# P V of a decode kernel: P standing in two column tiles, V moving, the useful quarter picked by 32-bit matmuls

## The chip, the cores and the metric

The kernel runs on one core of a Trainium2 chip. The metric is device microseconds of one execution, the median of three runs; beside it stands one execution taken with the hardware profiler, whose trace gives the durations used here. TensorE is called PE (its weight loads PEld), VectorE DVE, ScalarE ACT, GpSimd POOL; SP is the engine that issues nearly all DMAs. Times in the text are in us from the start of the profiled span, if nothing else is said.

## What is computed

One decode step of a block: attention over a window of cached keys and values, and then an MLP, each with a layer norm in front of it. Eight sequences (B = 8), one token each, D = 512; 32 query heads of 128, 8 KV heads, four query heads to each; the last W = 2048 positions of the cache.

```python
W = min(4096, max(256, Sk // 4))                      # 2048
q = (x @ wq).reshape(B, 1, 32, 128)                   # per head
k = k_cache[:, :, Sk - W:, :]; v = v_cache[:, :, Sk - W:, :]   # repeated for 4 heads each
p = softmax(q k^T * 128**-0.5)
attention = (p v) @ wo
h = x + attention(layernorm(x))
out = h + mlp(layernorm(h))     # its token shift is zero for one token, so w1 and w2 are not used;
                                # mlp(y) = y + gelu(layernorm(y) @ w3) @ w4, with F = 1792
```

K and V of the window are 67 MB of the 79.2 MB that the kernel reads.

## The kernel before, in words

**Units.** A unit n is one batch element b and one half t of its KV heads: n = 2 b + t, 16 units in all. Each has J = 4 KV heads, W = 2048 positions, and 2 MB of K and 2 MB of V. In SBUF a unit's K or V is one buffer `[128, 8192]`: partition 4 r + j holds, for KV head j, 64 positions of 128 numbers. There are four such buffers for K (`knat`) and four for V (`vnat`). "Even unit" below means t = 0 and "odd unit" t = 1.

**K.** PE turns a unit's K in four steps (`turn_K`, L296: eight 32-bit transposes each, reading two bf16 numbers as one), alternating between two PSUM buffers `kT_ps`; ACT empties the lower half of each (L283) and DVE the upper half (L284). After two such steps `pe_QK` (L311) multiplies: q standing with 32 columns, K moving with 512, in four column tiles of the array, one for each KV head. The scores of a batch element fill one PSUM bank, one row for each pair of head and position group.

**Softmax.** After the odd unit: the row maximum on DVE (`softmax_1`), matmuls that bring it together over partitions and back (`softmax_2`, L325, and `softmax_3`, L336), the exponential on ACT (L342). In the next even unit `softmax_spread` (L355, four steps on DVE) spreads P over four times its width with zeros in the other KV heads' places, `softmax_5` (L372, L375, L381) makes the reciprocal sums, and `softmax_4` (L364) turns P into `pS`, so that positions lie on partitions.

**P V.** `pe_PV(i)` is a quarter w of unit n (i = 4 n + w): 16 matmuls in which a chunk of V stands (128 x 128) and 16 columns of `pS` move, all 64 of a unit adding into `oT_ps[:, 0:16]`, so that the head dimension comes out on partitions. `scale` (L407, DVE) multiplies by the reciprocal sums and spreads the result in `oK`; `turn_o` (L417, four matmuls in column tiles; L422, a copy on DVE) rearranges it into `o2`, the moving operand of the product with wo (`pe_wo`, L458).

**Order.** Each engine gets its instructions in the order in which the program emits them, and waits on counters. One pass of the main loop handles K of unit n and P V of unit n - 3 (no P V in pass 14, unit 11 in pass 15):

```python
turn_K(i); spread(0); turn_os(pv[0] // U); turn_K(i + 1); spread(1); turn_K(i + 2); spread(2)
pe_QK(2 * n)
if t == 0 and b >= 1: softmax_5(b - 1)
turn_K(i + 3); spread(3); pvs(1)
pe_QK(2 * n + 1)
if t == 0 and b >= 1: softmax_4(b - 1)
if t == 1: softmax_1(b); pvs(2); softmax_2(b); pvs(3); softmax_3(b)
pvs(4)
```

`spread` does something in even units alone, and `pvs(k)` emits P V quarters up to the k-th of its unit. So an even unit has one quarter ahead of its second QK and three together at its end; in an odd unit the four stand apart. After the loop come the spreads of the last batch element, P V of unit 12, `softmax_5`, `softmax_4`, P V of units 13 to 15 with the first half of the product with wo among them, `turn_o` of unit 15, the second half of wo, and the MLP.

**DMA.** SP issues in program order: K of unit n waits until K of unit n - 4 has been turned, V of unit n until P V of unit n - 4 is done. V of unit 15 is issued in four pieces, behind it four pieces of wo, then w3 and w4 (these two into K's buffers). `sm` is a PSUM bank that L325, L336, L372 and `turn_o` share; a variable `sm_read` makes each of them wait for the last reader of it.

Of the kernel before, what the change touches and what calls it, by code (L numbers as in the profile page):

```python
# [6 lines left out]
dt = mybir.dt  # L7
ACT = mybir.ActivationFunctionType
ALU = mybir.AluOpType
AX = mybir.AxisListType  # L10
# [3 lines left out]
H = 32  # L14
DH = 128
G = 8
R = H // G
# [11 lines left out]
NU = 2  # L29
J = G // NU  # L30
U = 4
# [5 lines left out]
NV = 4  # L37
NKT = 4
LVD = 3
WO_AT = (5, 9)  # L40
WO_G = (0, 2)
WO_L = 4
QW = 12 + R + 28
SPR = 4


# [30 lines left out]
def bass_sequential_preLN__sliding_block_cached__mixer_s_mlp__decode_kernel(  # L77
# [19 lines left out]
    NUN = NB * NU  # L97
# [4 lines left out]
    with es:  # L102
        sb = lambda shape, dtype, name: es.enter_context(nc.sbuf_tensor(name, shape, dtype))
# [4 lines left out]
        vnat = sb([128, NV, UL], dt.bfloat16, "vnat")  # L108
# [6 lines left out]
        ident_f = sb([128, 128], dt.float32, "ident_f")  # L115
# [3 lines left out]
        sel_f = sb([128, H], dt.float32, "sel_f")  # L119
# [32 lines left out]
        mK = sb([128, R], dt.float32, "mK")  # L152
        rLk = sb([128, 2, H, R], dt.float32, "rLk")
        oK = sb([128, 2, J, R, R], dt.bfloat16, "oK")
        o2 = sb([128, G, R, B], dt.bfloat16, "o2")

        NH = KC * B
        tail = Pz[:, 0, :].bitcast(dt.float32)
        at = [0]
# [30 lines left out]
        def dma(eng, dst, src, sem, *waits):  # L190
            def f(e):
# [25 lines left out]
        e_sel = DV.op(lambda e: e.tensor_reduce(sel_f[:, :].rearrange("p (j h) -> p j h", j=J),  # L217
                                                ident_f[:, :].rearrange("p (j u h) -> p j h u", j=J, u=U),
                                                AX.X, ALU.add), e_idf)
        e_mE = DV.op(lambda e: e.tensor_reduce(mE[:, :], ident_f[:, :].rearrange("p (e k) -> p e k", k=R),  # L220
                                               AX.X, ALU.max))
        e_mK = DV.op(lambda e: e.tensor_reduce(mK[:, :], ident_f[:, :].rearrange("p (e k) -> p k e", k=R),
# [41 lines left out]

        def fill_q(b):
            for c in range(2):
                at = 12 + 16 * c
                e_qw[b] = PO.op(lambda e, c=c, at=at: e.tensor_copy(  # L268
                    qz[64 * c:64 * (c + 1), b % 2, :, :, at:at + R],
                    q_sb[64 * c:64 * (c + 1), :, :, b].rearrange("p k (g h) -> p g k h", h=R)),  # L270
                    e_qs, (PO.sem, PO.count), e_QK.get(2 * (NU * (b - 2) + 1) + 1))
# [30 lines left out]
        def pe_QK(m):  # L302
            n, v = divmod(m, 2)
            b, t = divmod(n, NU)
            lo = 12 - 8 * v - 4 * t
            kT = kT_sb[:, (2 * m) % NKT:(2 * m) % NKT + 2, :].rearrange("p u (c j r k) -> p j k (u c) r", c=8, j=J, k=2)

            def f(e):
                for k in range(2):
                    for j in range(J):  # L310
                        ins = e.matmul(S_ps[b % 2][32 * j:32 * (j + 1), :].rearrange("p (c r) -> p c r", c=16),  # L311
                                       qz[:, b % 2, J * t + j, k, lo:lo + 32], kT[:, j, k],
                                       start=(t == 0 and v == 0 and k == 0), stop=(t == NU - 1 and v == 1 and k == 1),
                                       tile_position=(0, 32 * j), skip_group_check=True)
                return ins
            e_QK[m] = PE.op(f, *e_ev[2 * m], *e_ev[2 * m + 1], e_qw[b], e_qs, e_exp.get(b - 2))
# [7 lines left out]
        def softmax_2(b):  # L324
            e_mT[b] = PE.op(lambda e: e.matmul(sm[0:1, MROW], mcol[:, :], ident_f[:, :], start=True, stop=True),  # L325
                            e_max[b], sm_read[0], e_idf)
            e = DV.op(lambda e: e.tensor_reduce(Mrow[:, :].rearrange("o (j h) -> o j h", j=J),  # L327
                                                sm[0:1, MROW].rearrange("o (j u h) -> o j h u", j=J, u=U),
                                                AX.X, ALU.max), e_mT[b])
            sm_read[0] = e  # L330
            m_bc = bass.AP(tensor=Mrow[:, :].tensor, offset=0, ap=[[H, 1], [8, J], [0, U], [1, 8]])
            e_neg[b] = DV.op(lambda e: e.tensor_scalar(negrow[:, :].rearrange("o (j u h) -> o j u h", j=J, u=U), m_bc,  # L332
                                                       -1.0, None, ALU.mult), e, e_negps.get(b - 1))

        def softmax_3(b):
# [46 lines left out]

        def V(n, w):
            if n == NUN - 1:
                return sem_vl[w], 16
            return sem_v[n % NV], 16 * (n // NV + 1)

        def pe_PV(i):
            n, w = divmod(i, U)
            b, t = divmod(n, NU)  # L390
            dst = oT_ps[:, 0:16]

            def f(e):
                for c in range(16):
                    o = (8 * (w % 2) + c // 2) * 128 + 16 * (2 * (2 * (c % 2) + w // 2) + t)
                    mvg = pS[:, b % 2, o:o + 16]
                    ins = e.matmul(dst, vnat[:, n % NV, (16 * w + c) * DH:(16 * w + c + 1) * DH], mvg,  # L397
                                   start=(w == 0 and c == 0), stop=(w == U - 1 and c == 15),
                                   skip_group_check=True)
                return ins  # L400
            e_PV[i] = PE.op(f, V(n, w), *e_pS[b], e_sc.get(n - 1))

        def scale(n):
            b, t = divmod(n, NU)
            src = oT_ps[:, 0:16]
            s_bc = bass.AP(tensor=src.tensor, offset=src.offset, ap=[src.ap[0], [1, 16], [0, R]])
            e_sc[n] = DV.op(lambda e: e.tensor_tensor(oK[:, n % 2].rearrange("p g r k -> p (g r) k"), s_bc,  # L407
                                                      rLk[:, b % 2, 16 * t:16 * t + 16, :], ALU.mult),
                            e_rL[b], e_PV[U * n + U - 1], e_scale.get(n - 2))

        def turn_o(n):
            b, t = divmod(n, NU)
# [19 lines left out]
        def load_v(n):  # L432
            b, t = divmod(n, NU)
            src = A_v_cache[b, J * t:J * (t + 1), W0:SK, :].rearrange("j (r c) d -> r j (c d)", r=RR)
            if n < NUN - 1:
                dma(SP, vnat[:, n % NV, :], src, sem_v[n % NV], e_PV.get(U * (n - NV + 1) - 1))
                return
            for w in range(U):
                cs = slice(w * UL // U, (w + 1) * UL // U)
                dma(SP, vnat[:, n % NV, cs], src[:, :, cs], sem_vl[w], e_PV.get(U * (n - NV + 1) - 1))  # L440

# [32 lines left out]
        turned = [0]  # L474

        def turn_os(to):
            while turned[0] < to:
                turn_o(turned[0])
                turned[0] += 1
# [6 lines left out]
        for n in range(NUN):  # L486
            if n < NUN - 1:
                load_k(n)
            if n == NUN - 2:
                load_k(n + 1)  # L490
            if n >= LVD:
                load_v(n - LVD)
            if n in WO_AT:
                load_wo(WO_G[WO_AT.index(n)], sem_wo)
            i = U * n
            b, t = divmod(n, NU)
            lag = LVD + (n >= NUN - 2)
# [85 lines left out]
        e = PE.op(lambda e: e.matmul(st2, ones_v[:, :], vsum[:, :], start=True, stop=True), e_vs, e_sc[NUN - 1])  # L583
# [72 lines left out]
```

## Time and profile before

| | |
|---|---|
| median of 3 runs | 197.72 us (197.44 to 197.91) |
| the profiled execution | 197.34 us |
| its span | 196.0 us |
| mean granted clock of PE | 0.872 |
| PE busy | 153.8 us (78%), 2415 matmul rows |
| DVE busy | 98.2 us (50%) |
| ACT busy | 85.9 us (44%) |
| P V (L397) | 1024 matmuls, 33.2 us busy |
| DMA | 79.18 MB read, 404 GB/s over the span |

A row of the timeline has the start, the time until its last part ended, engine and line, operation, what it writes and reads, partitions x elements, the number of instructions, and in brackets the engine's idle time before it with what ended it. Ends of matmuls are modelled and overlap with the next start, so the pace of PE is read from start to start. A 32-bit matmul of the program that is not a transpose shows as two rows. In the slices of the page a digit is a tenth, and PEclk is the granted clock.

### The profile page before, as it was taken

Reading aid. Unit: us, or ns where it says so; the run is one execution under the profiler, and the core shown is the slowest. Engines: PE = TensorE matmul, PEld = TensorE weight load, DVE = VectorE, ACT = ScalarE, POOL = GpSimd, SP = SyncE. Lnnn points to the kernel's source line nnn. Section 1 sums busy time; section 2 is a strip of 40 time slices with the busy share of each in tenths; the row PEclk is TensorE's granted clock in tenths of the full one; section 3 lists DMA queues with packets and bytes.
Section 4 is the critical chain, followed back from the end, with each engine's and each line's share of the span. In section 5 each row is a group of like instructions: output and inputs, shape, how many; then the busy total and the mean of one; then the engine's idle time right before and its main releaser. Section 6 shows DMA issues by size and latency. Waiting matters only on the chain.

```text
span 196.0 us, 5301 instructions
## 1 busy us (share of the span) xinstructions
PE 153.8 (78%) x2415; PEld 125.9 (64%) x2415; DVE 98.2 (50%) x223; ACT 85.9 (44%) x100; POOL 7.0 (4%) x28
## 2 busy tenths in 40 slices
PE   0038985978989898989885789898989897888464
PEld 0037852765869577868773668586958585777453
DVE  5302444865484566548553384549455765620130
ACT  6001565764456374735471355535635482230030
POOL 4001001001000100010001000100000000000000
PEclk9999999999699999997999579969997999555555
DMA  6999999999999999999999999999999999999970
GB/s 229 461 408 431 425 431 431 421 428 425 423 420 422 431 425 428 423 425 428 419 427 421 431 428 425 428 425 428 425 428 421 423 421 428 407 405 407 406 285 24
DMA packets 7542, 79.52 MB, mean 406 GB/s; under 512 B 856, under 2 KB 864, under 8 KB 3424
## 3 DMA queue, kind: packets, MB, share of 16 engines
q1 hardware_dynamic: 7504, 79.18, 96.1%
q8 instruction: 19, 0.31, 0.6%
q14 instruction: 3, 0.02, 0.0%
q10 hardware_dynamic: 16, 0.01, 0.0%
HBM read 79.18 MB, written 0.01 MB: 404 GB/s over the span
## 4 chain that ended last, share of the span: by engine, by line
DMA 51%; PE 31%; DVE 10%; SPq 5%; issue 2%
DMA knat<-in_A_k_cache_dram 42%; PE kT_ps L296 21%; DMA knat<-in_B_w_dram 9%; SPq L192 5%; PE S_ps L311 5%; DVE kT_sb L284 5%; DVE Pz L355 2%; PE kT_ps L364 2%; DVE mcol L321 1%; PE oT_ps L397 1%; PE sm L325 1%; PE sm L336 1%; DVE Mrow L327 1%; PE S_ps L607 1%; DVE negrow L332 0%
## 5 line engine op out<-in xcount | busy, mean ns | idle before, releaser
L283 ACT ACTIVATE kT_sb<-kT_ps 128x1024 bf16<-128x1024 bf16 x64 | 63.8, 1024 | 47.2 <-PE kT_ps L296 46.5
L296 PE MATMUL kT_ps<-perm_k,knat 128*128 128x128 f32 x512 | 76.1, 306 | 3.4 <-DMA knat<-in_A_k_cache_dram 3.2
L296 PEld LDWEIGHTS kT_ps<-perm_k,knat 128*128 128x128 f32 x512 | 65.7, 159 | 9.1 <-issue 4.3
L284 DVE TENSOR_SCALAR kT_sb<-kT_ps 128x512 int32<-128x512 int32 x64 | 44.2, 690 | 35.0 <-PE kT_ps L296 34.8
L397 PEld LDWEIGHTS oT_ps<-pS,vnat 128*128 128x128 bf16 x1024 | 30.5, 98 | 6.4 <-issue 6.1
L397 PE MATMUL oT_ps<-pS,vnat 128*128 128x16 bf16 x1024 | 33.2, 171 | 1.3 <-DVE oK L407 1.3
L311 PE MATMUL S_ps<-kT_sb,qz 128*32 128x512 bf16 x256 | 20.0, 386 | 11.0 <-DVE kT_sb L284 10.6
L355 DVE TENSOR_TENSOR Pz<-P_sb,mJ 128x512 bf16<-128x512 bf16 x32 | 21.6, 684 | 0.0
L342 ACT ACTIVATE P_sb<-S_ps,negcol 128x512 bf16<-128x512 f32 x8 | 5.5, 688 | 24.9 <-DVE negcol L339 24.9
L283 ACT ACTIVATE pS<-kT_ps 128x1024 bf16<-128x1024 bf16 x8 | 8.2, 1024 | 15.8 <-PE kT_ps L364 15.8
L311 PEld LDWEIGHTS S_ps<-kT_sb,qz 128*32 128x32 bf16 x256 | 4.7, 94 | 15.8 <-ACT kT_sb L283 14.8
L284 DVE TENSOR_SCALAR pS<-kT_ps 128x512 int32<-128x512 int32 x8 | 5.5, 692 | 9.4 <-PE kT_ps L364 9.4
L364 PEld LDWEIGHTS kT_ps<-perm_p,Pz 128*128 128x128 bf16 x128 | 8.1, 105 | 3.0 <-issue 3.0
L250 PE MATMUL S_ps<-xlnT,wbig 128*128 128x8 bf16 x128 | 3.6, 168 | 7.7 <-DMA wbig<-in_A_wq_dram 7.7
L364 PE MATMUL kT_ps<-perm_p,Pz 128*128 128x128 bf16 x128 | 9.4, 231 | 0.0
L407 DVE TENSOR_TENSOR oK<-oT_ps,rLk 128x64 bf16<-128x64 f32 x16 | 3.6, 224 | 11.1 <-PE oT_ps L397 11.1
L268 POOL COPY qz<-q_sb 64x64 bf16<-64x64 bf16 x16 | 4.6, 290 | 119.7 <-PE S_ps L311 103.5
L321 DVE TENSOR_REDUCE mcol<-S_ps 128x1 f32<-128x512 f32 x8 | 5.5, 692 | 6.5 <-PE S_ps L311 6.5
L250 PEld LDWEIGHTS S_ps<-xlnT,wbig 128*128 128x128 bf16 x128 | 3.5, 104 | 7.7 <-issue 7.7
L584 ACT ACTIVATE Pz<-oT_ps,eps 128x8 f32<-128x8 f32 x1 | 0.3, 268 | 15.0 <-PE oT_ps L583 15.0
L458 PE MATMUL S_ps<-o,wbig 128*128 128x8 bf16 x128 | 4.0, 168 | 2.3 <-issue 2.0
L255 DVE TENSOR_SCALAR kT_sb<-S_ps 128x256 bf16<-128x256 f32 x1 | 0.4, 425 | 10.0 <-PE S_ps L250 10.0
(83 smaller groups left out, 73.3 us busy)
## 6 DMA issues: line engine op xcount, KB each, us to landing
knat<-in_A_k_cache_dram SPq DMA_DIRECT2D x16, 2048.0 KB, 28.9
vnat<-in_A_v_cache_dram SPq DMA_DIRECT2D x15, 2048.0 KB, 30.8
wbig<-in_A_wq_dram SPq DMA_DIRECT2D x1, 4096.0 KB, 12.2
wbig<-in_A_wo_dram SPq DMA_DIRECT2D x2, 1024.0 KB, 30.8
vnat<-in_A_v_cache_dram SPq DMA_DIRECT2D x4, 512.0 KB, 9.4
wbig<-in_A_wo_dram SPq DMA_DIRECT2D x4, 512.0 KB, 11.8
knat<-in_B_w_dram SPq DMA_DIRECT2D x4, 448.0 KB, 13.0
knat<-in_B_w_dram SPq DMA_DIRECT2D x3, 512.0 KB, 16.6
```

The source lines that it names most:

```text
L192: e.dma_start(dst, src).then_inc(sem, 16)
L250: ins = e.matmul(S_ps[0][:, h * B:(h + 1) * B], wq_v[:, kc, h * DH:(h + 1) * DH], xlnT[:, kc * B:(kc + 1) * B], start=(kc == 0), stop=(kc ...
L268: e_qw[b] = PO.op(lambda e, c=c, at=at: e.tensor_copy(qz[64 * c:64 * (c + 1), b % 2, :, :, at:at + R], q_sb[64 * c:64 * (c + 1), :, :, b]. ...
L283: e_lo.append(AC.op(lambda e: e.activation(dst[:, 0:1024], ps[:, 0:1024], ACT.Copy), e_Tlo[k], *free))
L284: e_hi.append(DV.op(lambda e: e.tensor_single_scalar(dst[:, 1024:2048].bitcast(dt.int32), ps[:, 1024:2048].bitcast(dt.int32), 0, ALU.bitwi ...
L296: ins = e.matmul(ps[:, c * 128:(c + 1) * 128], src[:, c * 128:(c + 1) * 128], perm_k[:, :], is_transpose=True)
L311: ins = e.matmul(S_ps[b % 2][32 * j:32 * (j + 1), :].rearrange("p (c r) -> p c r", c=16), qz[:, b % 2, J * t + j, k, lo:lo + 32], kT[:, j, k],
L321: e_max[b] = DV.op(lambda e: e.tensor_reduce(mcol[:, :], S_ps[b % 2][:, :], AX.X, ALU.max), e_QK[4 * b + 3], e_mT.get(b - 1))
L342: e_exp[b] = AC.op(lambda e: e.activation(P_sb[:, :], S_ps[s][:, :], ACT.Exp, bias=negcol[:, s:s + 1], scale=1.0, accum_out=lcol[:, s:s + 1]),
L355: e_Pz[b, part] = DV.op(lambda e: e.tensor_tensor(Pz[:, 0, J * w * part:J * w * (part + 1)].rearrange("p (x j) -> p x j", j=J), p_bc, m_bc ...
L364: ins = e.matmul(ps[:, c * 128:(c + 1) * 128], Pz[:, 0, c * 128:(c + 1) * 128], perm_p[:, :], is_transpose=True)
L397: ins = e.matmul(dst, vnat[:, n % NV, (16 * w + c) * DH:(16 * w + c + 1) * DH], mvg, start=(w == 0 and c == 0), stop=(w == U - 1 and c == 15),
```

## The change

P V changes its operands. 64 columns of `pS` now stand, and 512 columns of V, four chunks, move: each matmul yields 64 rows by 512 columns, of which only the quarter in which P's columns and V's chunk belong together is useful. A unit takes 16 such matmuls, in two column tiles of 64 that alternate, into the whole bank `oT_ps`. Each of the four quarters w of a unit is four matmuls. For this the order of the rows of the scores changes (`fill_q`, `lo`, and the views in `softmax_2`).

After a unit's last quarter ACT copies the bank to SBUF (`evict_o`, 128 x 512, 32 bits). `fold` then takes four 32-bit matmuls: the 128 columns of `oE` that belong to one chunk stand, and 16 columns of a 0/1 matrix `selo` move, which pick the useful rows and add the two tiles; the sum, in `sm[:, 32:48]`, has the form that `oT_ps[:, 0:16]` had, and DVE's product follows as before. P V of the next unit waits for the copy rather than for the product.

In the loop `fold_os` takes the place of `turn_os`, which moves behind the first `pe_QK`, ahead of `softmax_5`. After the loop, `fold` comes behind the first quarter of the next unit and `turn_o` behind its second; `pe_wo` of the first four groups is cut in two, the second of them behind the last P V. The four pieces of the last V are issued in the order 0, 2, 1, 3, and a quarter waits for two of them. `qz` becomes wider (56 columns for 44).

```diff
-QW = 12 + R + 28
+QW = 24 + 32
+VP = 2
+MO = 32 * VP
+NO = 256 * VP
+TO = 128 // MO
...
+        oE = sb([128, 512], dt.float32, "oE")
+        selo = sb([128, MO], dt.float32, "selo")
...
+        e_selo = DV.op(lambda e: e.tensor_reduce(selo[:, :], ident_f[:, :].rearrange("p (a x) -> p x a", a=TO),
+                                                 AX.X, ALU.add))
...
-                at = 12 + 16 * c
+                at = 24 + R * c
...
-            lo = 12 - 8 * v - 4 * t
+            lo = 24 - 16 * t - 8 * v
...
         def pe_PV(i):
             n, w = divmod(i, U)
             b, t = divmod(n, NU)
-            dst = oT_ps[:, 0:16]
+            v4 = vnat[:, n % NV, :].rearrange("p (v u c d) -> p u c v d", v=2, u=2, c=8)
 
             def f(e):
-                for c in range(16):
-                    o = (8 * (w % 2) + c // 2) * 128 + 16 * (2 * (2 * (c % 2) + w // 2) + t)
-                    mvg = pS[:, b % 2, o:o + 16]
-                    ins = e.matmul(dst, vnat[:, n % NV, (16 * w + c) * DH:(16 * w + c + 1) * DH], mvg,
-                                   start=(w == 0 and c == 0), stop=(w == U - 1 and c == 15),
-                                   skip_group_check=True)
-                return ins
-            e_PV[i] = PE.op(f, V(n, w), *e_pS[b], e_sc.get(n - 1))
-
-        def scale(n):
+                for c in range(4 * (w % 2), 4 * (w % 2) + 4):
+                    o = (8 * (w // 2) + c) * 128 + 64 * t
+                    q = c % TO
+                    ins = e.matmul(oT_ps[MO * q:MO * (q + 1), :].rearrange("p (v d) -> p v d", v=2), pS[:, b % 2, o:o + MO],
+                                   v4[:, w // 2, c],
+                                   start=(w == 0 and c < TO), stop=(w == U - 1 and c >= 8 - TO),
+                                   tile_position=(0, MO * q), skip_group_check=True)
+                return ins
+            e_PV[i] = PE.op(f, *V(n, w), *e_pS[b], e_ev_o.get(n - 1))
+
+        def evict_o(n):
+            e_ev_o[n] = AC.op(lambda e: e.activation(oE[:, :], oT_ps[:, :], ACT.Copy),
+                              e_PV[U * n + U - 1], e_fold.get(n - 1))
+
+        def fold(n):
...
+                for s in range(2 * VP):
+                    o = 128 * s
+                    ins = e.matmul(sm[:, 32:48], oE[:, o:o + 128], selo[:, 16 * s:16 * s + 16],
+                                   start=(s == 0), stop=(s == 2 * VP - 1))
+                return ins
+            e_fold[n] = PE.op(f, e_ev_o[n], e_selo, sm_read[0])
...
-            for w in range(U):
+            for w in (0, 2, 1, 3):
...
         def emit_PV(i):
-            if i % U == 1 and i > U:
-                turn_os(i // U)
-                if i // U == NUN - 1:
-                    pe_wo((0, 1, 2, 3), e_scale[NUN - NU], (sem_wo, 16 * len(WO_AT)))
+            n, w = divmod(i, U)
+            if w == 1:
+                fold_os(n)
+            if w == 2:
+                turn_os(n)
+                if n == NUN - 1:
+                    pe_wo((0, 1), e_scale[NUN - NU], (sem_wo, 16 * len(WO_AT)))
             pe_PV(i)
-            if i % U == U - 1:
-                scale(i // U)
+            if w == U - 1:
+                evict_o(n)
...
-            turn_os(pv[0] // U)
+            fold_os(pv[0] // U)
             turn_K(i + 1)
...
             pe_QK(2 * n)
+            turn_os(pv[0] // U)
             if t == 0 and b >= 1:
                 softmax_5(b - 1)
...
         emit_PVs(NBLK)
-        turn_o(NUN - 1)
+        pe_wo((2, 3))
+        fold_os(NUN)
+        turn_os(NUN)
```

More of the change, by code (lines that the diff above doesn't have):

```diff
@@ L215, in bass_sequential_preLN__sliding_block_cached__mixer_s_mlp__decode_kernel @@
                                                 ALU.subtract, ALU.mult), e)
-        e_sel = DV.op(lambda e: e.tensor_reduce(sel_f[:, :].rearrange("p (j h) -> p j h", j=J),
-                                                ident_f[:, :].rearrange("p (j u h) -> p j h u", j=J, u=U),
+        e_sel = DV.op(lambda e: e.tensor_reduce(sel_f[:, :].rearrange("p (j t h) -> p j t h", j=J, t=NU),
+                                                ident_f[:, :].rearrange("p (j t u h) -> p j t h u", j=J, t=NU, u=U),
                                                 AX.X, ALU.add), e_idf)
+        e_selo = DV.op(lambda e: e.tensor_reduce(selo[:, :], ident_f[:, :].rearrange("p (a x) -> p x a", a=TO),
+                                                 AX.X, ALU.add))
         e_mE = DV.op(lambda e: e.tensor_reduce(mE[:, :], ident_f[:, :].rearrange("p (e k) -> p e k", k=R),
@@ L326, in softmax_2 @@
                             e_max[b], sm_read[0], e_idf)
-            e = DV.op(lambda e: e.tensor_reduce(Mrow[:, :].rearrange("o (j h) -> o j h", j=J),
-                                                sm[0:1, MROW].rearrange("o (j u h) -> o j h u", j=J, u=U),
+            e = DV.op(lambda e: e.tensor_reduce(Mrow[:, :].rearrange("o (x h) -> o x h", h=R),
+                                                sm[0:1, MROW].rearrange("o (x u h) -> o x h u", u=U, h=R),
                                                 AX.X, ALU.max), e_mT[b])
             sm_read[0] = e
-            m_bc = bass.AP(tensor=Mrow[:, :].tensor, offset=0, ap=[[H, 1], [8, J], [0, U], [1, 8]])
-            e_neg[b] = DV.op(lambda e: e.tensor_scalar(negrow[:, :].rearrange("o (j u h) -> o j u h", j=J, u=U), m_bc,
+            m_bc = bass.AP(tensor=Mrow[:, :].tensor, offset=0, ap=[[H, 1], [R, NU * J], [0, U], [1, R]])
+            e_neg[b] = DV.op(lambda e: e.tensor_scalar(negrow[:, :].rearrange("o (x u h) -> o x u h", u=U, h=R), m_bc,
                                                        -1.0, None, ALU.mult), e, e_negps.get(b - 1))
@@ L384, in V @@
             if n == NUN - 1:
-                return sem_vl[w], 16
-            return sem_v[n % NV], 16 * (n // NV + 1)
+                return (sem_vl[w // 2], 16), (sem_vl[2 + w // 2], 16)
+            return ((sem_v[n % NV], 16 * (n // NV + 1)),)
+        e_ev_o, e_fold = {}, {}
         def pe_PV(i):
@@ L390, in pe_PV, with f @@
             b, t = divmod(n, NU)
-            dst = oT_ps[:, 0:16]
+            v4 = vnat[:, n % NV, :].rearrange("p (v u c d) -> p u c v d", v=2, u=2, c=8)
             def f(e):
-                for c in range(16):
-                    o = (8 * (w % 2) + c // 2) * 128 + 16 * (2 * (2 * (c % 2) + w // 2) + t)
-                    mvg = pS[:, b % 2, o:o + 16]
-                    ins = e.matmul(dst, vnat[:, n % NV, (16 * w + c) * DH:(16 * w + c + 1) * DH], mvg,
-                                   start=(w == 0 and c == 0), stop=(w == U - 1 and c == 15),
-                                   skip_group_check=True)
-                return ins
-            e_PV[i] = PE.op(f, V(n, w), *e_pS[b], e_sc.get(n - 1))
-        def scale(n):
-            b, t = divmod(n, NU)
-            src = oT_ps[:, 0:16]
+                for c in range(4 * (w % 2), 4 * (w % 2) + 4):
[5 more added lines that the diff above has]
+                                   tile_position=(0, MO * q), skip_group_check=True)
+                return ins
+            e_PV[i] = PE.op(f, *V(n, w), *e_pS[b], e_ev_o.get(n - 1))
[3 more added lines that the diff above has]
+        def fold(n):
+            b, t = divmod(n, NU)
+            def f(e):
+                for s in range(2 * VP):
[4 more added lines that the diff above has]
+            e_fold[n] = PE.op(f, e_ev_o[n], e_selo, sm_read[0])
+            src = sm[:, 32:48]
             s_bc = bass.AP(tensor=src.tensor, offset=src.offset, ap=[src.ap[0], [1, 16], [0, R]])
@@ L408, in scale @@
                                                       rLk[:, b % 2, 16 * t:16 * t + 16, :], ALU.mult),
-                            e_rL[b], e_PV[U * n + U - 1], e_scale.get(n - 2))
+                            e_rL[b], e_fold[n], e_scale.get(n - 2))
+            sm_read[0] = e_sc[n]
         def turn_o(n):
@@ L464, in emit_PV, with fold_os @@
         def emit_PV(i):
-            if i % U == 1 and i > U:
-                turn_os(i // U)
-                if i // U == NUN - 1:
-                    pe_wo((0, 1, 2, 3), e_scale[NUN - NU], (sem_wo, 16 * len(WO_AT)))
+            n, w = divmod(i, U)
[5 more added lines that the diff above has]
+                    pe_wo((0, 1), e_scale[NUN - NU], (sem_wo, 16 * len(WO_AT)))
             pe_PV(i)
-            if i % U == U - 1:
-                scale(i // U)
+            if w == U - 1:
+                evict_o(n)
         pv = [0]
         turned = [0]
+        folded = [0]
+        def fold_os(to):
+            while folded[0] < to:
+                fold(folded[0])
+                folded[0] += 1
         def turn_os(to):
@@ L581, in pe_w3 @@
             return ins
-        e = PE.op(lambda e: e.matmul(st2, ones_v[:, :], vsum[:, :], start=True, stop=True), e_vs, e_sc[NUN - 1])
+        e = PE.op(lambda e: e.matmul(st2, ones_v[:, :], vsum[:, :], start=True, stop=True), e_vs, e_ev_o[NUN - 1])
         e2 = AC.op(lambda e: e.activation(vv[:, 0:B], st2, ACT.Sqrt, bias=eps2[:, :], scale=1.0 + EPS), e)
```

## The prediction

> **What bounds the kernel now.** I read the page's 40 slices first, then the DMA queue's issues and landings, then TensorE's timeline.
>
> ```profile
> PE   0038985978989898989885789898989897888464
> PEclk9999999999699999997999579969997999555555
> DMA  6999999999999999999999999999999999999970
> ```
>
> The DMA row is full from the second slice to slice 38: 79.2 MB stream without a hole, and all but the last 3 us of the span lie under them. TensorE (PE) is second, at 8 to 9 tenths, so the question is how far it stands behind. The waits, and the rows of two stretches, say that:
>
> ```profile
> PE S_ps L311 <- DVE kT_sb L284: 10.6, 16, 1.2
> PE kT_ps L296 <- DMA knat<-in_A_k_cache_dram: 3.2, 2, 3.0
> ...
> 109.04 1.97 PE L296 MATMUL kT_ps<-perm_k,knat 128*128 128x128 f32 x8 [3.03 <-DMA knat<-in_A_k_cache_dram]
> ...
> 148.22 1.10 PE L296 MATMUL kT_ps<-perm_k,knat 128*128 128x128 f32 x8 [0.17 <-DMA knat<-in_A_k_cache_dram]
> ```
>
> PE waits for data only twice after it has begun: unit 10 and unit 14 of K start as they land (109.0, 148.2). PE therefore runs just at the pace of the stream: two units (2 of K, 2 of V, 8.39 MB) land every 19.6 us (K10, K12 and K14 at 109.0, 128.6 and 148.2), and PE needs the following for them (warm clock):
>
> ```profile
> 69.37 1.07 PE L296 MATMUL kT_ps<-perm_k,knat 128*128 128x128 f32 x8
> 70.38 0.19 PE L417 MATMUL sm<-oK,mE 128*32 128x16 bf16 x4
> 70.50 1.97 PE L296 MATMUL kT_ps<-perm_k,knat 128*128 128x128 f32 x16
> 72.70 0.62 PE L311 MATMUL S_ps<-kT_sb,qz 128*32 128x512 bf16 x8 [0.24 <-issue]
> 73.25 0.41 PE L372 MATMUL sm<-lsel,ones_f 128*128 128x32 f32 x2
> 73.49 1.07 PE L296 MATMUL kT_ps<-perm_k,knat 128*128 128x128 f32 x8
> 74.40 0.55 PE L397 MATMUL oT_ps<-pS,vnat 128*128 128x16 bf16 x16
> 75.74 0.62 PE L311 MATMUL S_ps<-kT_sb,qz 128*32 128x512 bf16 x8 [0.79 <-DVE kT_sb L284]
> 76.29 1.07 PE L364 MATMUL kT_ps<-perm_p,Pz 128*128 128x128 bf16 x16
> 77.19 1.35 PE L397 MATMUL oT_ps<-pS,vnat 128*128 128x16 bf16 x48
> ```
>
> From start to start this is an even unit: 69.37 to 78.40, 9.03 us. The odd one ends at 87.14: 8.74. Together 17.8, or 1.8 under the stream; but the clock falls to half for 3.4 us at the head of most even units (50.2, 87.7, 128.7, 149.2), which makes them 10.0 to 10.2, and the pair 18.7 to 18.9. About one microsecond per pair is all the room there is.
>
> Third, the tail. The end of P V of unit 11 lets SP issue the last V:
>
> ```profile
> 165.64 2.48 SPq L192 DMA_DIRECT2D vnat<-in_A_v_cache_dram  x4
> 166.01 0.56 PE L397 MATMUL oT_ps<-pS,vnat 128*128 128x16 bf16 x16 [0.41 <-DVE oK L407]
> 182.00 0.65 PE L458 MATMUL S_ps<-o,wbig 128*128 128x8 bf16 x18 [0.33 <-DVE o L422]
> 184.35 1.39 PE L458 MATMUL S_ps<-o,wbig 128*128 128x8 bf16 x46 [1.70 <-issue]
> ```
>
> V14 lands at 172.7, so that issue has some 7 us to spare, less the 1.4 us from issue to landing that even the 8 KB store takes. PE does P V of units 12 to 15 in the 15.5 us after 165.5; then it waits for the last wo chunk (landed 184.4), for w3 (188.9) and w4 (192.6, 193.3).
>
> **The change part by part.** Starts of rows are used, since ends overlap.
>
> *P V.* Before: 64 matmuls of 16 columns at a 25 ns pitch, 1.63 us a unit (0.41 for 16, 1.20 for 48, 77.19 to 78.40). After: 16 matmuls of 512 columns in two column tiles. The nearest row is L311, 512 columns in four tiles: eight start as two rounds, four rows 4 ns apart and the second four 0.205 later, and the block takes 0.55 to the next block (81.49 to 82.04). So two rounds are 0.43 plus 0.12 to empty the array. Taken over: a block of four is 0.55, the block of twelve 6 x 0.213 + 0.12 = 1.40. Bounds: 1.23 without the 0.12, and 2.68 if the two tiles take turns. The first P V block of a unit hides before L311's wait for VectorE (0.49 to 0.79 above), the next two of an odd unit behind the softmax steps (0.86 and 0.69 between starts, against 0.41 of work). Left: +0.20 in the even unit, +0.14 in the odd one.
>
> [...] The weights, 64 columns per matmul, would load under the running round, as L311's do.
>
> *Fold.* Four 32-bit matmuls, each two rows (L372: x2 for one matmul, 0.24 to the next block, 92.28 to 92.52). 4 x 0.24 = 0.96; from L296's 109 ns per 32-bit row 0.87; at the half clock 8 x 0.235 (L562) = 1.9. I take 0.95, on PE, once per unit, between turn_K(i) and turn_K(i+1).
>
> *Copy.* ScalarE 128x512 from PSUM, 0.69 as L342. In the loop turn_K(i), 1.0 on PE, covers it, except in even units, where it queues behind the exponential: fold then waits 0.3. The K copies queue behind it by 0.7, less than PE is later. In the tail nothing covers it: P V of the next unit waits for it, some 0.85 from block to block against 0.47 for VectorE's product now.
>
> *turn_os moves behind pe_QK.* Its 0.12 stays. But softmax_5, next on PE, waits for the copy of turn_o on VectorE, as both use sm; that copy is now queued behind the third spread. PE's queue behind it holds turn_K(i+3), P V, QK and the turn of P. The waits show one such case, after the loop:
>
> ```profile
> PE sm L372 <- DVE o L422: 0.9, 1, 0.9
> ```
>
> Even unit from its start, after: turn_K 0 to 1.0; fold 1.3 to 2.25; two turns to 4.1; QK to 4.65; turn_o to 4.8. VectorE (0.6 per step): K copy 3.25, spread 3.85, K copy 4.45, spread 5.05, turn_o's copy 5.65 to 5.9. L372 at 5.95, so 1.15 idle; turn to 7.1; its copy 7.2 to 7.8; QK at 7.95 (6.37 before); P turn 8.5; twelve P V 9.4 to 10.8. Against 9.03: +1.77. Odd unit: +0.95 fold, +0.14 P V, -0.1 for ScalarE's wait at QK that the fold covers: 9.7. The pair: 20.5.
>
> *The clock.* Working out the streamed columns of every 3.4 us window (32-bit ones of L296 twice, by their 109 ns), the clock fell after windows with at most 34% of streaming time and rose only after 85% or more. The windows that fell hold three P V blocks of 0.1 us streaming each (16 x 16 columns); these become 0.43 each, near 60% in all. So I count the loop as warm, which is why 20.5 stands against 17.8 and, net, against 18.8.
>
> [...]
>
> *Loop sum.* Unit 3 ends at 50.6 (50.5). Then five pairs of 20.5: unit 14 starts at 153.2 (148.2 before), 5.0 late; its K landed long ago, so PE no longer waits. Unit 14 has no P V: 9.4 (8.8, half cold, before). Unit 15: 8.6 (8.45). P V 11 ends at 171.2, 5.7 later than 165.5. The last V starts by about 173 against 172.7: DMA loses under 1 us, which the following hides.
>
> *Tail sum.* Copy of unit 11 waits for the exponential: P V 12 from 172.5, with fold to 175.75 (0.55 + 0.95 + 0.55 + 0.13 + 0.97 for two blocks together, 3.15 a unit, and 0.1 for turn_o); L372 and P turn to 176.9; P V 13 to 180.05, copy wait 0.85; P V 14 to 184.05, wait 0.85; P V 15 with 36 wo matmuls (27 ns each) and its wait for turn_o 1.35: 189.4; 32 more 190.25; fold, product, turn, copy 2.0: 192.25; 64 wo matmuls 1.75: 194.0. The sum at L559 starts at 194.15, 8.4 later than 185.77. Behind it, 10.25 before, the waits for w3 and w4 are gone: the last w4 matmuls come 1.9 sooner after it (w3 can start 0.6 after L583, then ScalarE's table load and two Gelus set the pace). End: 194.15 + 8.35 = 202.5, and 0.5 for a fold in the half clock. Span 203.0 against 196.0, +7.0. The profiled execution took 197.34 (1.34 around the span), the median 197.72; 204.3 to 204.7. I say 204.4.
>
> The rest is free: the wider qz fill (0.3 on GpSimd) and selo's reduction (0.3 on VectorE) lie ahead of 13.1, when wq lands; ScalarE's load of the Sqrt table, now behind the last copy, is done 4 us before L584.
>
> **The rivals.**
> *DMA still sets the end.* Mechanism: PE's pair stays within 19.6 and its tail ends P V 15 by about 181.6, where wo's landing takes over. For it: the full DMA row. Fewer instructions (some 1280 of 5301) also shorten the instruction queue (0.31 MB, 0.6%), about 0.3 us. Then 197.4 to 197.7. Against: it needs 8 us less PE work than my sum.
> *PE keeps pace, the tail pays.* If the wait at L372 doesn't come or rows are shorter, the pair is under 19.6 and unit 14 starts at 148.2 again; the tail is 5.0 sooner: 199.4.
> *Half clock in the tail.* Between copies and folds the streaming share is 31 to 44%, at the edge of 34. Once down, P V is +1.7 and fold +0.9 a unit; three units: 212.
> *The tiles take turns.* Twelve in 2.68 and four in 0.97: the pair 22.7, PE 16 late at unit 14, the tail 1.7 more for each of four units: 222.
>
> **How the numbers follow.** My sum 0.60, pace kept 0.14, half clock 0.12, turns 0.06, DMA 0.08. Measurement tells 0.2%, 0.4 us. The DMA rival gives 0.05 for the same and 0.03 for faster; slower 0.92. The range runs from pace kept, 199.0, to half clock, 212.5; it leaves out DMA and turns, 0.14.
>
> **What would show it.** In the profile after: P V blocks at 0.55 and 1.40; fold rows x8 at 0.95; an idle of about 1.1 before L372's successor in even units, released by VectorE's copy of o2; no wait of L296 for K at units 10 to 14; PEclk without dips until the tail; the DMA row thinning from slice 38; the sum before w3 released by wo matmuls, not landings. Waits of L296 for K with DMA full to the end would prove me wrong, as would pair times under 19.6.

## The result and the profile after

| | before | after |
|---|---|---|
| median | 197.47 us (197.25 to 197.91, 6 runs) | 206.58 us (202.98 to 212.36, 6 runs) |
| profiled execution | 197.34 us, span 196.0 | 207.72 us, span 206.4 |
| mean granted clock of it | 0.872 | 0.943 |
| end of P V of unit 11 | 165.5 us | 170.57 us |
| matmul rows of the trace | 2415 | 1775 |

The ratio is 1.0322, with an interval of 1.0258 to 1.0386. It leaves out the three runs of after that are more than 1.5% above its quickest, the profiled one among them, so it sits below the quotient of the medians. The runs of after lie far apart, and nearly in the order of their clock: 202.98 us (0.976), 203.25 (0.977), 205.45 (0.960), 207.72 (0.943), 210.39 (0.932), 212.36 (0.919).

The 40 slices of the changed kernel:

```profile
PE   0048896798799879987999799979996887889875
PEclk9999999999999999999999999999999999975555
DMA  7999999999999999999999999999999986999300
```

Before, DMA was full to slice 38 and the clock dipped at the head of most even units. Now the clock holds until slice 35, and DMA thins in slices 33 and 34 and is empty two slices before the end: PE sets the end. Two groups are to be read for the prediction's steps (busy us, mean ns of one, idle before and its releaser):

```profile
L407 PE MATMUL oT_ps<-vnat,pS 128*64 128x512 bf16 x256 | 39.6, 410 | 2.6 <-ACT oE L415 2.6
L380 PE MATMUL sm<-lsel,ones_f 128*128 128x32 f32 x16 | 3.3, 286 | 7.5 <-DVE o L446 7.5
```

The new P V is itself no quicker than the old one: 39.6 us busy against 33.2, and from start to start 0.55 + 1.42 = 1.97 us in an even unit against about 1.6. L380 has a wait that its predecessor did not have in the loop. Starts tell more. Unit 10 and the first blocks of unit 11 in the timeline:

```profile
111.69 1.09 PE L304 MATMUL kT_ps<-perm_k,knat 128*128 128x128 f32 x8
112.12 0.59 ACT L415 ACTIVATE oE<-oT_ps 128x512 f32<-128x512 f32 x1
112.76 1.06 PE L424 MATMUL sm<-selo,oE 128*128 128x16 f32 x8
113.67 1.94 PE L304 MATMUL kT_ps<-perm_k,knat 128*128 128x128 f32 x16
...
116.01 0.21 PE L441 MATMUL sm<-oK,mE 128*32 128x16 bf16 x4
117.19 0.22 DVE L446 CAST o<-sm 128x16 bf16<-128x16 f32 x1
117.46 0.41 PE L380 MATMUL sm<-lsel,ones_f 128*128 128x32 f32 x2 [1.24 <-DVE o L446]
...
121.22 1.49 PE L407 MATMUL oT_ps<-vnat,pS 128*64 128x512 bf16 x12
122.64 1.09 PE L304 MATMUL kT_ps<-perm_k,knat 128*128 128x128 f32 x8
123.57 0.96 PE L424 MATMUL sm<-selo,oE 128*128 128x16 f32 x8
```

The copy (112.12) lies under turn_K; its 16 rows average 0.593 us. The fold takes 0.91 us in the even unit (112.76 to the next turn at 113.67) and 0.81 in the odd one (123.57 to 124.38). `turn_o` (116.01) is done early, but VectorE is in a spread when it ends and copies at 117.19; L380, the first matmul of `softmax_5`, waits 1.24 us for that. Twelve P V matmuls take 1.42 (121.22 to 122.64). The even unit is 10.95, this pair 20.46 (111.69 to 132.15), against a stream of 19.6.

The tail, PE alone:

```profile
182.58 1.74 PE L407 MATMUL oT_ps<-vnat,pS 128*64 128x512 bf16 x8
185.11 1.06 PE L407 MATMUL oT_ps<-vnat,pS 128*64 128x512 bf16 x4 [0.78 <-ACT oE L415]
186.10 1.89 PE L424 MATMUL sm<-selo,oE 128*128 128x16 f32 x8
...
198.30 0.60 PE L598 MATMUL sm<-Pz,ones_m 128*128 128x8 f32 x2 [0.28 <-DVE Pz L595]
```

L598 is the first matmul of the layer norm behind the product with wo; it is called the sum below. The clock halves at 182.8, within the first of these rows, and never rises again: a fold of 1.0 becomes 1.8 (186.10 to the next row at 187.92). The changes of the clock in the traces lie whole multiples of 3.41 us apart, so its windows can be laid out. Counted from the starts of the rows (512 columns in 0.213 us at the full clock; a round of column tiles once, as the rounds of the twelve at 121.22 start 0.216 apart; 32-bit columns twice, as 128 of them take 0.109 in L304's rows), the columns that PE streamed in the window from 179.4 were 35% of what the full clock would stream, and in the window before it 59%. The window from 169.1 had 35% too, and the clock held behind it.

### The profile page after: what moved, and what is told of

It is laid out like the page before. It is cut to its first block, busy times and chain, and to the rows that moved or that the text cites. A ratio compares the mean times of both kernels' runs of the same rounds, so it can differ in the third digit from the quotient of the medians.

```text
span 206.4 us, 4045 instructions
## 1 busy us (share of the span) xinstructions
PE 166.4 (81%) x1775; PEld 114.5 (55%) x1775; DVE 99.8 (48%) x224; ACT 93.6 (45%) x116; POOL 7.3 (4%) x28
## 4 chain that ended last, share of the span: by engine, by line
PE 64%; DVE 22%; DMA 8%; issue 3%; ACT 2%; SPq 0%; DVEq 0%
PE kT_ps L304 27%; DVE kT_sb L292 10%; PE oT_ps L407 10%; DMA knat<-in_A_k_cache_dram 8%; PE sm L424 8%; PE S_ps L319 7%; DVE Pz L363 6%; PE kT_ps L372 4%; DVE mcol L329 3%; PE S_ps L482 2%; PE sm L333 2%; PE sm L344 1%; PE sm L380 1%; DVE Mrow L335 1%; DVE negrow L340 1%
## 5 line engine op out<-in xcount | busy, mean ns | idle before, releaser
L304 PE MATMUL kT_ps<-perm_k,knat 128*128 128x128 f32 x512 | 67.2, 282 | 0.2
L304 PEld LDWEIGHTS kT_ps<-perm_k,knat 128*128 128x128 f32 x512 | 58.6, 147 | 8.9 <-issue 7.8
L407 PE MATMUL oT_ps<-vnat,pS 128*64 128x512 bf16 x256 | 39.6, 410 | 2.6 <-ACT oE L415 2.6
L415 ACT ACTIVATE oE<-oT_ps 128x512 f32<-128x512 f32 x16 | 9.5, 593 | 22.2 <-PE oT_ps L407 22.2
L407 PEld LDWEIGHTS oT_ps<-vnat,pS 128*64 128x64 bf16 x256 | 10.7, 112 | 15.2 <-issue 11.7
L424 PEld LDWEIGHTS sm<-selo,oE 128*128 128x128 f32 x128 | 17.1, 208 | 3.3 <-issue 1.6
L424 PE MATMUL sm<-selo,oE 128*128 128x16 f32 x128 | 18.2, 275 | 0.0
L430 DVE TENSOR_TENSOR oK<-sm,rLk 128x64 bf16<-128x64 f32 x16 | 3.5, 222 | 15.6 <-PE sm L424 15.1
L380 PE MATMUL sm<-lsel,ones_f 128*128 128x32 f32 x16 | 3.3, 286 | 7.5 <-DVE o L446 7.5
L372 PEld LDWEIGHTS kT_ps<-perm_p,Pz 128*128 128x128 bf16 x128 | 7.3, 98 | 3.0 <-issue 3.0
L372 PE MATMUL kT_ps<-perm_p,Pz 128*128 128x128 bf16 x128 | 8.5, 220 | 0.0
```

Of the source, the lines that this page charges most:

```text
L304: ins = e.matmul(ps[:, c * 128:(c + 1) * 128], src[:, c * 128:(c + 1) * 128], perm_k[:, :], is_transpose=True)
L372: ins = e.matmul(ps[:, c * 128:(c + 1) * 128], Pz[:, 0, c * 128:(c + 1) * 128], perm_p[:, :], is_transpose=True)
L380: e_Lb[b] = PE.op(lambda e: e.matmul(sm[:, LB], ones_f[:, :], lsel[:, :], start=True, stop=True), e_lsel[b], sm_read[0])
L407: ins = e.matmul(oT_ps[MO * q:MO * (q + 1), :].rearrange("p (v d) -> p v d", v=2), pS[:, b % 2, o:o + MO], v4[:, w // 2, c], start=(w == 0 ...
L415: e_ev_o[n] = AC.op(lambda e: e.activation(oE[:, :], oT_ps[:, :], ACT.Copy), e_PV[U * n + U - 1], e_fold.get(n - 1))
L424: ins = e.matmul(sm[:, 32:48], oE[:, o:o + 128], selo[:, 16 * s:16 * s + 16], start=(s == 0), stop=(s == 2 * VP - 1))
```

## The experiments

Each asks which part carries the loss: the place of `turn_o`, the fold's 32 bits, the fold at all, or the clock. Kernels that ran on the same chip share their runs of before (medians of it 197.44, 197.42 and 197.35 us).

### turn_o back in its old place

```diff
             turn_K(i + 1)
+            turn_os(pv[0] // U)
             spread(1)
...
             pe_QK(2 * n)
-            turn_os(pv[0] // U)
```

> The changed kernel with turn_os moved from behind pe_QK(2n) to behind turn_K(i+1), so that its copy on VectorE stands ahead of the second spread and is done before softmax_5 asks for sm. Loop theory (TensorE's pair of units, 20.4 us against 19.6 of the stream, puts unit 14 off by 4.4 us, and the end follows): TensorE's idle before L380 goes from 1.2 us to under 0.2, the even unit from 10.9 to about 9.6, the pair to 19.1, unit 14 starts at 148 to 149 instead of 152.6, and the time falls by about 4.4 us, to 198.5 to 199.5. Tail theory (copies and folds behind unit 11 set the end by themselves): the pair falls as well, but the time stays within 1 us of 203.

202.78 us (201.23 to 204.5); 1.0246 of before [1.0204, 1.0288]. Its slices and its PE timeline:

```profile
PEclk9999999999999999999999999999999996798555
```

```profile
112.54 0.62 PE L319 MATMUL S_ps<-kT_sb,qz 128*32 128x512 bf16 x8
113.09 0.41 PE L380 MATMUL sm<-lsel,ones_f 128*128 128x32 f32 x2
...
166.77 1.45 PE L424 MATMUL sm<-selo,oE 128*128 128x16 f32 x8
...
169.27 1.92 PE L407 MATMUL oT_ps<-vnat,pS 128*64 128x512 bf16 x8
```

In the loop the mechanism is as expected: L380 follows QK with no wait, the pair is 19.66 us (88.76 to 108.42), unit 14 starts at 148.14 as its K lands (148.1), and P V of unit 11 ends 5.5 us sooner, at 165.05. The time is not: it missed the 198.5 to 199.5 of the loop theory and lies where the tail theory had it, within 1 us of 203. The median is 3.8 us under after's, but the quickest run, 201.23, only 1.8 under after's quickest. In the tail of the trace the clock fell at 167.3, after a window with 30% of columns streamed, came back at 174, and fell again at 184 (28%); a fold then takes 1.4 to 1.9, and eight P V matmuls 1.92 for 1.05. The expectation had priced the place at a full clock. So it is tried again below with the clock held, which decides between the two theories.

### The fold in 16 bits

```diff
-        oE = sb([128, 512], dt.float32, "oE")
-        selo = sb([128, MO], dt.float32, "selo")
+        oE = sb([128, 512], dt.bfloat16, "oE")
+        selo = sb([128, MO], dt.bfloat16, "selo")
```

(The reduction that makes `selo` takes a maximum in place of a sum, which is the same for zeros and a one.)

> The changed kernel with oE and selo in 16 bits, so that the fold is four matmul rows of 16 bits instead of eight of 32. Loop theory: the fold falls from 0.91 to about 0.15 us, the pair to about 18.9, unit 14 starts at 148.2 as its K lands; in the tail four folds save 3 us more, so the landing of the last w4 sets the end again: 197.4 to 198.2. Tail theory: only the tail's folds count, about 3.5 us off 203: 199.5.

197.01 us (196.28 to 200.92); 0.9979 [0.996, 0.9998]: the loss is gone, with the copy, the selection and the place of `turn_o` as in after. From its PE timeline:

```profile
149.05 0.25 PE L424 MATMUL sm<-selo,oE 128*128 128x16 bf16 x4
149.15 1.95 PE L304 MATMUL kT_ps<-perm_k,knat 128*128 128x128 f32 x16
...
153.41 0.41 PE L380 MATMUL sm<-lsel,ones_f 128*128 128x32 f32 x2 [1.26 <-DVE o L446]
```

Four rows in 0.10 us, where eight took 0.81 to 0.91; the copy, now into 16 bits, still takes 0.597. The wait before L380 is still there (1.26), but the pair is 19.2 us (68.71 to 87.93), below the stream, and unit 14 starts at 148.12, when K has landed. A wait of 1.26 costs little once the fold leaves room for it: the kernel below that takes it out as well is 0.95 us quicker.

### No copy and no fold

```diff
-            e_ev_o[n] = AC.op(lambda e: e.activation(oE[:, :], oT_ps[:, :], ACT.Copy), ...)
+            src = oT_ps[:, 0:16]
+            e_sc[n] = DV.op(...)        # the product, straight from PSUM
+            e_ev_o[n] = e_sc[n]
...
         def fold(n):
+            return
```

> The changed kernel without the copy of the bank and without the fold: VectorE's product takes the first 16 columns of the bank directly, so the picking and adding of the useful quarter is left out. It gives the price of P V in two column tiles and of the later turn_o alone. If copy and fold are what costs: the even unit about 10.1 (the wait before L380 stays), the odd one 8.6, pair 18.7, and the end on the last landing: 197.2 to 198.0. If the column tiles or the later turn_o cost by themselves: over 199.5.

196.02 us (195.84 to 196.82); 0.9926 [0.991, 0.9943]. This is 1.2 us under what was expected, as the last w4 lands at 191.96 here (193.27 in before). The pair is 18.95 us (68.55 to 87.50), under the stream, with `turn_o` as late as in after. So the new P V and the later `turn_o` without copy and fold make a kernel that is not slower than the old one, and without the picking of the useful quarter there is no loss. This doesn't make the picking the only part of it: with the 32-bit fold in place, the later `turn_o` has a price too, as the first experiment and a later one show. Against the 16-bit fold it is one microsecond better, so that fold and its copy cost little.

### Before, with the clock held in the loop

```diff
             pvs(2)
+            warm(n, 2)
             softmax_2(b)
             pvs(3)
+            warm(n, 1)
```

`warm(n, k)` adds k matmuls of 496 columns, in odd units alone, into the unused part of `oT_ps`.

> The kernel before, with three matmuls of 496 columns whose result nobody reads put into the waits of each odd unit (two behind the second P V quarter, one behind the third). If the granted clock follows the streamed share of a window (down at 34% or less): no dips of the clock at the heads of the even units any more, even unit 9.0 instead of 10.0, pair 17.8. If the stream of data sets the end: the time stays at 197.5 within 0.4 us all the same. If the dips cost the kernel time: 196.5 or less. If the clock falls for another reason: dips stay.

197.33 us (197.28 to 197.45 in nine of its ten runs, 266.99 in one); 0.999 [0.9977, 1.0003]. Its slices:

```profile
PEclk9999999999999999999999589999996999755555
```

The dips at 50, 88 and 129 us are gone; those at 107.7 and 148.7, where PE waits for K, remain. DMA is full to slice 38 as in before. Units 4 to 7 are 8.8 to 9.0 us each (17.85 a pair, 50.33 to 68.18), as the prediction had worked out for a warm clock, and PE then waits for K of unit 10, which lands at 108.9. The dips that are gone had cost before nothing, and the warm clock that the change brought to the loop was worth nothing by itself.

### After, with the clock held in the tail

```diff
             if w == U - 1:
                 evict_o(n)
+                if NUN - 5 <= n < NUN - 1:
+                    PE.op(warm, e_hi[70], e_lo[70])   # 3 matmuls of 512 columns into a free bank
```

> The changed kernel with three matmuls of 512 columns, which nobody reads, behind the last P V quarter of units 11 to 14, where TensorE waits for the copy of the bank (0.85 us and more). Clock theory (what spreads the changed kernel's runs from 203.0 to 212.4 is whether a 3.4 us window of the tail falls to about 35% streamed columns): every run at 202 to 203.5, clock at half only from about 185 on. If the clock in the tail follows something else: the spread of 203 to 212 stays. If the fill itself delays P V: all runs 1 to 2 us over 203.

203.91 us (203.65 to 204.71); 1.0329 [1.0302, 1.0356]. Slices and PE timeline:

```profile
PEclk9999999999999999999999999999999999999955
```

```profile
184.97 0.62 PE L407 MATMUL oT_ps<-vnat,pS 128*64 128x512 bf16 x4
...
194.57 0.60 PE L604 MATMUL sm<-Pz,ones_m 128*128 128x8 f32 x2 [0.28 <-DVE Pz L601]
```

This fits the clock as what spreads the runs of after. The fills stand where PE would wait for the copy; no window falls under 42% until 189.9, and the four runs lie within 0.5% of one another, where after's six span 4.6%. They all lie above the 202 to 203.5 expected, and none is quicker than after's quickest, 202.98. P V of unit 15 starts at nearly the same time in the two traces (184.97 and 185.11); then the sum comes at 194.57 against 198.30 (L598 there). These 3.73 us are the whole difference of the spans, 206.4 and 202.7. The half clock cost more than that: from the row at 182.58, whose counterpart here starts at 183.13, to the sum it is 15.72 against 11.44 us, 4.28 more, but this kernel came to that row 0.55 later, as a fill holds L380 back. Only one run of after has a trace, so for its other runs the clock is argued from their granted clocks.

### Both: turn_o early and the clock held

> The early turn_os (first edit) together with the filled tail, the fold still in 32 bits. Loop theory with the clock held: the early turn_os brought P V of unit 11 to 165.1, 5.5 us ahead of the changed kernel, but the clock fell at 167 in its tail; with the clock held the tail takes the 31 us of the changed kernel's quickest runs: 197.3 to 198.5. Tail theory (the tail has its length whatever the loop does, and the clock is not the reason): 201 to 204.

The edits of the first and the fifth experiment together: 200.6 us (199.34 to 201.45); 1.015 [1.0108, 1.0191]. Its PE timeline:

```profile
165.47 0.82 PE L502 MATMUL kT_ps<-pS,ident_b 128*128 128x512 bf16 x3
...
190.29 0.60 PE L604 MATMUL sm<-Pz,ones_m 128*128 128x8 f32 x2 [0.28 <-DVE Pz L601]
```

Against the fifth experiment the place of `turn_o` is worth 3.3 us of the medians, 4.3 of the profiled spans (198.38 against 202.67): P V of unit 11, whose end is where the first fill starts, ends 5.1 sooner (165.47 against 170.57), and the sum comes 4.3 sooner (190.29 against 194.57). So most of the loop's lag does pass to the end, as the sum of the prediction had it. The time missed what was expected: the median lies 2 us above the loop theory's range and under the tail theory's, and two of the four runs (201.41 and 201.45) lie in the latter. The fold of unit 15 ran at half clock here (2.19 us from its start to the next matmul, against 1.43), and a fill holds L380 back by 0.66, as it does in the fifth experiment too.

### turn_o early and the fold in 16 bits

> Both of the first two edits together: turn_os behind turn_K(i+1), and the fold in 16 bits. Loop theory: the pair is about 17.6, so unit 14 starts as its K lands (148.1) and P V of unit 11 ends at 165.2, 3.2 us ahead of the 16-bit fold alone; the last V is then issued before the queue runs empty, and the end hangs on the last landing (192.0): 195.6 to 196.4. If the end of the 16-bit fold alone already hung on the landing: 196.8 to 197.2.

196.06 us (195.81 to 196.28); 0.9925 [0.9907, 0.9943]: 0.75% under before, as the loop theory had it. Its PE timeline:

```profile
180.05 1.92 PE L407 MATMUL oT_ps<-vnat,pS 128*64 128x512 bf16 x8
...
186.11 0.60 PE L598 MATMUL sm<-Pz,ones_m 128*128 128x8 f32 x2 [0.28 <-DVE Pz L595]
```

The pair is 18.6 us (69.12 to 87.69), PE waits for K again, and the clock falls in the tail at 179.5 (a row of eight P V matmuls takes 1.92 us for 1.05) without harm: the sum is at 186.1, and the last w4 lands at 191.74.

### Why the last landing is earlier than before's

In the last kernel PE is no longer what ends, and yet it comes out under before. Its last landing is 191.74, before's 193.27, with the same bytes. K of unit 14 landed at 148.15 and 148.17 us and the last V at 177.8 and 177.9, so the difference arises behind that. The queues of before and of this kernel differ in instruction packets of 16 KB, 19 and 13; one such packet takes some 1.05 us on its DMA engine, one of 8 KB 0.31. Two kernels add instructions on other engines: the third experiment with 80 small writes of GpSimd in each unit, and the kernel above with 116 waits of SP, already fulfilled, in each of units 2 to 12.

> The kernel without copy and fold, with 80 small memsets per unit on GpSimd, which is otherwise idle: 1280 instructions more, as many as the change took from TensorE. It asks why the kernels with P V in tiles get their last data at 192.0 and the one before at 193.3, with the same 79.2 MB. Fetch theory (instruction packets share the DMA engines with the data; 13 and 14 packets of 16 KB against 19): packets back to 18 or 19, last landing back to about 193.2, time 197.0 to 197.5. If the number of instructions doesn't matter: last landing 192.0, time 195.8 to 196.8.

> The kernel with the early turn_os and the 16-bit fold, with 116 waits on SP in each of units 2 to 12, on a counter that has long passed (1276 instructions, no data touched by them); the DMA queue is 24 us ahead, so the issues themselves are not late for it. Padding GpSimd with memsets had delayed the landing of K by 3.3 us at unit 10. Fetch theory (each instruction packet takes its time from the stream of data; 10 packets of 8 KB at 0.31 us): packets rise by about 10, K10 lands 2 to 3.4 us later than 107.9, the last data at 194 to 195, time 198 to 199.5. If GpSimd's writes into SBUF had slowed the data: K10 at 107.9, last data at 191.7, time 196.1 as without the waits.

```profile
q14 instruction: 13, 0.11, 0.1%
```

```profile
q14 instruction: 8, 0.07, 0.1%
```

The first line is of the GpSimd kernel, the second of the SP kernel; both had 3 such packets without the edit. With GpSimd's writes: 199.53 us (199.19 to 199.95), 1.0098 [1.007, 1.0127], 3.5 above the kernel without them; K of unit 10 lands at 111.0 (107.7), K of unit 14 at 151.4 (148.1), the last w4 at 195.56. With SP's waits: 196.05 (195.97 to 196.08), 0.9931 [0.9914, 0.9948], no different; K of unit 10 at 109.2 (107.9), but K of unit 14 at 148.3 (148.1) and the last landing at 191.9. GpSimd's kernel is slower than either theory had it. SP's has the time and the last landing that its second theory gave (GpSimd's writes as the cause), but not that theory's K of unit 10. And it adds half of what was planned: its trace shows 638 instructions more (4555 for 3917), not 1276, and five packets, not ten. From 40 us on its issues come up to 2.9 us later too (a V at 42.85 for 39.96), so the packets need not be what delays unit 10. Whether GpSimd's packets or its writes delayed the stream for good isn't told apart. Nor is the 1.5 us at the end: before's trace has four instruction packets between 169 and 188, this kernel's two, and a third at 189.7, which fits. Against it, the first experiment has one from 169 to its last landing, at 188.0, and there as here the last w4 lands 14.0 us behind the last V (15.4 in before). Packets in the tail alone were not tried.

## Why the prediction was right, and where it was off

**P V** was taken from QK's rows: 0.55 for a block of four and 1.40 for twelve; measured 0.55 (180.36 to 180.91) and 1.42. The 0.12 that both sums add to the rounds, called the emptying of the array there, is a gap that the rows show: in after the rounds of the twelve start 0.216 apart, the second 0.02 later than that, and the next block 0.10 later (121.22 to 122.63). In before, rows without column tiles have none (L364 to L397 0.056 us, as from row to row of L364). The tiles run side by side (the two rows of a round start 4 ns apart), so the rival in which they take turns (2.68) is out.

**Fold**: 0.95 predicted, 0.91 and 0.81 measured. The bound from the 32-bit transposes, 0.87, was the better row. **Copy**: 0.69 from the exponential of the same shape, 0.593 measured; the wait before the fold in even units was 0.1 for 0.3. In the tail each copy costs 0.78 for 0.85.

**The wait at L372's successor**: 1.15 predicted, 1.24 measured, by the releaser named, VectorE's copy of `o2` behind the third spread. The first experiment, which removes it alone, shows that it is the place of `turn_o` that makes it.

**The clock in the loop** stayed up, as the count of streamed columns had it: from 22.4 to 169.1 no window of after is under 40%. In the traces of before and after the granted clock has two rates, 1.0 and 0.5. A long wait is not needed for a fall: after's clock fell at 182.8 behind a window with 35% of the columns streamed, and the only wait of PE in it was 0.78 us. The prediction's 34% is not a sharp edge either: after's clock held behind 35% at 169.1.

**Loop sum**: even unit 10.8, odd 9.7, pair 20.5; measured 10.93, 9.48 (units 4 and 5) and 20.41. Unit 14 was to start at 153.2 (50.6 and five pairs make 153.1) and P V of unit 11 to end at 171.2; measured 152.56 and 170.57. The last V was issued at 170.67, and the last landing came 1.3 us later than before (194.56 for 193.27), hidden as said, if by a little more than the 1 us allowed. The DMA row was to thin from slice 38; it thins in slices 33 and 34 already (368 and 194 GB/s), around the issue of the last V.

**Tail sum**: 31.8 us from there to the end of the span. In after's quickest run the span was 201.7; if its loop took what the profiled one did, the tail was 31.1. With the clock held by fills the sum comes at 194.57, for 194.15, and the span is 202.7. The 203.0 was thus right for a run whose clock holds.

**The term that was too small is the last one**, "0.5 for a fold in the half clock". In the profiled run the half clock cost 4.28 us up to the sum alone, and the median of six, 206.58, is 2.2 above the forecast. "Half clock in the tail" was a rival with 0.12; it is rather a matter of degree. By their granted clocks (0.976 and 0.977, as in the kernel whose clock is held) the two quickest runs escape it, the slowest (212.36, at 0.919) is at the 212 that the rival gave, and the others lie between. That where the windows of 3.41 us fall decides this from run to run is likely, but not shown, as one run was traced. How near a median of six comes to 204.4 is then in part luck.

**The instruction queue** was counted at 0.3 us. This bears on nothing in after, where the end is PE's; where DMA sets it, the landing was 1.5 us earlier (191.74 against 193.27), of a cause that stays open.

## What to carry to other kernels

Before swapping the operand that stands for the one that moves, price what brings the result into its old form, in the data type in which it will run: here the kernel without picking was no slower, and taking the picking in four 16-bit rows for eight of 32 bits (0.10 us against 0.81 to 0.91 a unit) took the loss away. When a step moves behind another in one engine's queue, look up where the engine that answers it is by then; `turn_o`, of 0.12 us, cost 1.24. And where PE waits in turns with short work, count streamed columns in the clock's windows: here the clock fell behind windows of up to 37.5% and held behind others from 34.9% on. Filler in the waits brought the spread of the runs from 4.6% to 0.5% in one kernel; with `turn_o` early it was 1.1%.

## What was not expected of the hardware

The clock fell not only where PE stood still: its rows covered 77% of the window from 179.4 in after. Counted alike in all eleven traces, it fell behind 29 windows of 0 to 37.5% of the columns that the full clock would stream, and held behind 461 of 34.9% and more: in these traces the edge lies between 35 and 37.5%, as sharp as the count is (37.5% from 145.8 in before, 34.9% from 169.1 in after). It rose again only behind windows of 82% and more of what the half clock would stream; 75% was not enough (in before 84.5% from 128.7 was, 65% from 108.2 was not). And K of unit 10 lands at 107.5 to 107.9 us in the kernels with 13 or 14 packets of 16 KB and none added on other queues, but at 109.0 and 108.9 in the two with 19, at the same bytes of data. This is not a stream that is behind for good: K of unit 14 lands at 148.0 to 148.5 us in all of these.
